# Last output rows of two batches as one tile of 128 rows, and a new order of all instruction lists

## The chip, the cores and the metric

The kernel runs on one core of one Trainium2 chip. The core has a matrix engine (TensorE, "PE" in the profile, with its weight loads as "PEld"), a vector engine (DVE), a scalar engine (ACT), GpSimd (POOL), a queue for transfers (SyncE, "SP"), and 16 DMA engines that move data. The engines run their own lists of instructions, each list in its order, and wait for one another by semaphores. The metric is the device time of one execution in microseconds, as the median of several runs.

## The reference

Eight batches, eight heads, 576 positions, 64 features a head. First a linear attention with cosine weights, then a gated long convolution of the attention's output:

```
# attention, per batch and head
theta = pi/2 * pos / S
phi(x) = concat(relu(x)*cos(theta), relu(x)*sin(theta))      # 128 features
kv  = phi(k)^T v            # 128 x 64
z   = sum_s phi(k)          # 128
att = phi(q) kv / (phi(q) z + 1e-6)

# gated convolution, per batch; x = att with heads side by side: 576 x 512
x1, x2, x3 = split(x @ w_proj)                               # 512 -> 3 * 512
x2_conv    = irfft(rfft(x2, n=S) * rfft(filter_fft, n=S))    # along the 576 positions
out        = (x1 * x2_conv * x3) @ w_out                     # 576 x 512, float32
```

## The kernel before, in words

All matrix products are in float16 with float32 sums in PSUM. PSUM is used in four units of 4 KB a partition (`unit`, line 69); every product goes into a unit, and an eviction (`ev`, line 131, on ACT, or on DVE where the plan says so) or a DVE operation empties it. The next product but three needs that unit again.

For each batch b the work is cut into steps, each with a two- or three-letter name:

- `Lq`, `Lk`, `Lv`: loads of q, k, v (`load_rows`, line 156) from POOL's queue, which turn float32 into float16. There are six raw buffers, so a load of batch b waits until batch b-2 has been used.
- `pk`, `pq` (lines 505 and 519): the products relu(k)·cos, relu(k)·sin and those of q, in pieces, on DVE, or on ACT where the word has `'a`. `va` copies v.
- `kv` (line 556): kv and z by 40 small matmuls. `qt` (573): q's features transposed, by PE for batches 0 and 1 and by a DMA transpose from SP's queue after that. `num` (600): numerator and denominator, then three DVE operations that end in `att`.
- `fx` (629): the folding of positions that begins the Fourier transform. `xp` (666) and `xt` (659): att transposed, by PE for batches 0 to 2, by a DMA transpose for batches 3 to 7. `pr` (676): x2 = the folded att times w_proj, the largest 512-column products. `dft` (701), `mul` (718), `inv` (765): transform, product with the filter's spectrum, inverse transform.
- `ga`, `gb` (730): x1 and x3 from xt and w_proj, 8 matmuls of 288 columns for each of four blocks. `g` (751): their product.
- `y` (786): the last steps of the inverse transform and the product with the gates. It leaves `y` for rows 0 to 511 of the batch in four groups of 128 columns, and `ye` for the last 64 rows.
- `out` (837): the output product. `out b.0` and `out b.1` make two tiles of 128 rows each, evict 128x1024 float32 and store two times 256 KB. `out b.2` is for the last 64 rows (`left`, line 853): since 64 rows fill half of the array, columns 0 to 255 go to partitions 0 to 63 and columns 256 to 511 to partitions 64 to 127, by two matmuls of 256 columns for each of four blocks of the sum; then a 128x256 eviction and two stores of 64 KB. Batch 7 is done tile by tile (`end`, line 863).

The order is written out by hand: a text of words (line 905), and `run` (line 890) takes the next step of each word's generator when the word comes. So `out0.2` in three places means: matmuls, eviction, store. `*3` means three steps, `'a` ACT, `'v` DVE, and `~` that a load is held until the last DVE operation and transpose issued so far. Each engine's list is the order in which the words name its steps.

Buffers that matter here: `att`, `xt`, `y`, `ye` and `g` two each; `os` (the output of a full eviction) three; `os4` (that of the last rows) one.

Of the kernel before, what the change touches and what calls it, by code (L numbers as in the profile page):

```python
# [11 lines left out]
FP32 = mybir.dt.float32  # L12
FP16 = mybir.dt.float16
# [4 lines left out]
def kernel(  # L18
# [19 lines left out]
    nc = tc.nc  # L38
# [3 lines left out]
    B, NH, S, D = q.shape  # L42
    DM = NH * D
    NJ = 5
    NP = 96
    NC = DM // 128
# [7 lines left out]
    OUTSC = 2.0 ** -29  # L54
# [5 lines left out]
    NM = NC * 128  # L60

# [5 lines left out]
    late = {}  # L67
# [26 lines left out]
    wo16 = const("wo16", [128, NC, DM], FP16)  # L94
# [691 lines left out]
    def step_y(b, c, n):  # L786
# [10 lines left out]
        if "y" not in moe[b]:  # L797
# [9 lines left out]
            out=ym[:, :, :, 0:128], in0=ym[:, :, :, 0:128],  # L807
# [3 lines left out]
        if "ye" not in moe[b]:  # L811
            moe[b]["ye"] = late["p"].tile([128, NC, 64], FP16, tag="ye", bufs=2, name=f"ye{b}")
        tt(
            out=moe[b]["ye"][:, c : c + n].rearrange("p c (a t) -> p c a t", t=4),
# [5 lines left out]
    def out_tile(b, t, dst, cs):  # L820
        y = moe[b]["y"]
        for c in cs:
            if t < 4:
                nc.tensor.matmul(  # L824
                    dst, y[:, c, ds(QS * t, 128)], wo16[:, c], start=(c == 0), stop=(c == NC - 1),
                )
                continue
            for hf in range(2):
                nc.tensor.matmul(
                    dst[ds(64 * hf, 64), 0 : DM // 2], moe[b]["ye"][:, c],  # L830
                    wo16[:, c, ds(hf * (DM // 2), DM // 2)], start=(c == 0), stop=(c == NC - 1),
                )
# [20 lines left out]
    def left(b, u):  # L853
        os_ = late["p"].tile([128, DM // 2], FP32, tag="os4", bufs=1, name=f"os{b}_4")
# [35 lines left out]
    def run(plan, **batch):  # L890
# [15 lines left out]
        cols io0 pad1 Sk0.0 pad2 cols io2 rows io1 cols rows th tf warm0.12 cols*5 Sv0.0  # L906
        rows pad0 th'v rows*3 th'v cols*3 rows pk0.0'a*2 rows pk0.0'a*2 tf pk0.0 rows
        pk0.0'a tf pk0.0 cols*2 rows va0.1 cols ones0 rows*2 pk0.0*2 rows va0.0'v pk0.0'a
        th'v Lq0.0 Lq0.1 kv0.0 rows pq0.0 pq0.0'a*4 pq0.0 pq0.1*2 qt0.1 pq0.1*3 Lk0.1 qt0.0
        pq0.1'a qt0.2 kv0.0 qt0.1'b num0.1 tf pk0.1'a pk0.1*3 tf pk0.1 qt0.0'c num0.0 pk0.1  # L910
        ones1 pk0.1'a pk0.1*2 Lv0.1 va0.2 num0.0 num0.1 pk0.1'a va0.3'v qt0.2'b Lw0 kv0.1*2
        num0.1 num0.0 num0.1 cols Lw2 num0.0 qt0.3 rows Lq1.2 num0.2*2 cols*2 xp0.0 qt0.3'b
        rows num0.2 rows num0.2 Lk1.2 xp0.0*2 xp0.0'a num0.3*4 xp0.1 Lv1.2 ga0.0 gb0.3 Lw1
        xp0.1*2 pad4 cols pad5 ti xp0.1'v cols pad3 Lf gb0.0*2 tf ga0.0 gb0.0 ga0.0 Lf
        gb0.3*2 ga0.3 gb0.2 ti tf th ~Lq2.2 cols ~Lk2.2 cols pq1.2*2 pq1.2'a pq1.2*2 pq1.2'a
        rows gb0.2 ga0.3 ga0.1*2 ga0.3'v ti cols fx0.1 fx0.0 pk1.2 gb0.2 pk1.2 gb0.1*2 ga0.1
        fx0.3 fx0.1 pk1.2*2 fx0.0'v ga0.2 pk1.2 fx0.2 th gb0.1 fx0.3 fx0.2 ga0.2*2 pk1.2
        tf'v pk1.2*4 qt1.0 va1.0'v kv1.2 va1.1'v kv1.2 th kv1.2 qt1.1 g0.0.2 qt1.0'v th
        ~Lq3.1 tf qt1.0'v qt1.1'v qt1.2 qt1.1'v qt1.2 ~Lk3.0 qt1.2 num1.0*3 tf pr0.1 th
        num1.1 num1.0 num1.2 g0.2.2 num1.1 tf ~Lq3.0 num1.2 num1.1 pr0.1 tf ti pr0.0 num1.2  # L920
        num1.1 qt1.3 num1.2 pr0.0 pr0.2 qt1.3 dft0.0 feo0 pr0.2 dft0.0 feo1 h0 qt1.3'v xp1.0
        ti xp1.0 pq2.2 fx1.1 pq2.2 h0'v h1 ~Lv2.2 pq2.2 xp1.0 pq2.2 pk2.2 xp1.0'v pk2.2
        pk2.2'a h0 fx1.1 pk2.2 num1.3*3 pq2.2 num1.3 pq2.2 qt2.3 h2 qt2.0 fx1.2 h1 pk2.2 h1
        pk2.2 xp1.1 fx1.3 xp1.1 ~Lk3.1 ~Lq4.1 ~Lv3.1 h2 fx1.2 xp1.1'v fx1.3 xp1.1'v fx1.0
        pk2.2*2 dft0.1 dft0.1'v ~Lo dft0.2 ga1.0 fx1.0 dft0.2 mul0 ti mul0 pr1.0 pr1.2 ti*2
        mul0 ga1.0 mul0 pr1.1 pr1.1'v pr1.0 ga1.0 inv0.1 inv0.0 ~Lq4.0 ti pk2.2 late pr1.2
        dft1.2 dft1.0 dft1.2'v inv0.1 dft1.1 pk2.2 inv0.0 inv0.2 va2.0'v dft1.0 kv2.2 pq3.2
        va2.1'v inv0.3 kv2.2 y0.0.2 ~Lk4.1 y0.0.2 dft1.1 inv0.2 ga1.2*2 mul1 gb1.2 mul1
        qt2.1 kv2.2 num2.0 ~Lv3.0 qt2.2 num2.0 inv0.3 num2.1 pq3.2'a ga1.2 gb1.2 ~Lv4.0
        num2.1 num2.0 num2.1 num2.0 num2.1 gb1.3*2 mul1*2 gb1.2 gb1.1*2 pq3.2'a pq3.2 gb1.3  # L930
        pq3.2'a ga1.1 pk3.2 gb1.1 num2.2 ~Lk4.0 num2.2*3 y0.0.2 ga1.1 y0.0.2 fx2.1 y0.2.2
        ga1.1 y0.2.2 gb1.0*2 pk3.2'a fx2.1 inv1.1 fx2.2 pk3.2 gb1.0 inv1.1 fx2.2 ga1.3
        y0.2.2 ga1.3 inv1.0 inv1.0'v ga1.3 xp2.0 num2.3*3 xp2.0*3 num2.3 pk3.2 inv1.3*2
        y0.0.2 inv1.2*2 fx2.0*2 fx2.3*2 g1.0.2 ga2.0 xp2.1*2 pr2.0 xp2.1*2 pq3.2 ga2.0
        y0.2.2 qt3.0 va3.0'v y1.0.2 pk3.2 pk3.2'a*2 pk3.2 y0.2.2 pk3.2'a pq4.2 pr2.1 ga2.0
        qt3.2 pq4.2 out0.0 pr2.2 pr2.1 pr2.0 out0.0 dft2.1 y1.0.2 dft2.0 ~Lq5.0 va3.1'v
        y1.0.2 ~Lq5.1 ~Lv4.1 y1.0.2 pk3.2 ~Lv5.0 qt3.1 y1.2.2*2 pr2.2'v dft2.1 y1.2.2 dft2.2
        kv3.2*2 y1.0.2 gb2.1 y0.2.2 gb2.1 dft2.0 g1.2.2 y0.0.2 pq4.2'a ~Lv5.1 qt3.3 dft2.2'v
        kv3.2 gb2.0*2 mul2*2 num3.0*4 ~Lk5.0 gb2.1 gb2.0 gb2.3 pk4.2'a gb2.3*2 ~Lk5.1 out0.2
        ga2.2*2 fx3.0 out0.2 pq4.2'a ga2.1 mul2*2 ga2.2 fx3.0 num3.1*2 num3.2*2 pk4.2'a  # L940
        ga2.1 num3.1 pk4.2 out0.1 num3.2 num3.1 y1.2.2 ga2.1 num3.2 num3.3*2 pk4.2 pk4.2'a
        num3.3*2 ga2.3 gb2.2 ga2.3 xt3 pq4.2'a gb2.2 out0.1 fx3.1 fx3.2 ga2.3 inv2.1 gb2.2
        fx3.3 pq4.2 qt4.0 qt4.1 pk4.2'a pk4.2*2 fx3.3 fx3.1'v fx3.2'v inv2.1 pk4.2'a inv2.0
        pk4.2 inv2.0 g2.2.2 qt4.2 va4.0'v va4.1'v y2.0.2*2 pr3.0*2 pr3.1 pq5.2 pr3.1 kv4.2
        g2.0.2 y1.2.2 ~Lk6.0 ~Lq6.0 kv4.2*2 pq5.2'a pr3.2 ga3.0 pk5.2 pr3.2'v pk5.2 y1.2.2
        ga3.0 inv2.2 out0.2 dft3.2 ~Lk6.1 inv2.2'v dft3.0*2 dft3.2'v dft3.1*2 num4.0 inv2.3
        pk5.2*2 inv2.3 num4.0 y1.0.2 pq5.2'a gb3.1 num4.1 num4.0*2 num4.2 mul3 gb3.1 num4.1
        ~Lq6.1 pq5.2'a out1.0*2 num4.2 num4.1 pq5.2'a qt4.3 num4.1 ga3.1*2 pq5.2'a y2.0.2
        num4.2 gb3.0 num4.2 y2.0.2 y2.2.2 num4.3 gb3.0 num4.3 out0.0 out1.1*2 y2.2.2 num4.3
        gb3.3 fx4.0 qt5.2 num4.3 fx4.2 gb3.2 mul3 xt4 gb3.3'v ga3.2 qt5.1 mul3 pk5.2 fx4.0  # L950
        fx4.2 mul3 fx4.1 g3.0.2 inv3.0 qt5.0 gb3.2 qt5.3 fx4.3 y2.2.2 ga3.2 fx4.1 pk5.2*3
        inv3.0'v fx4.3 pk5.2 inv3.1 inv3.1'v y2.2.2 y3.0.2*2 pk5.2'a pr4.0 y3.0.2 inv3.3
        pr4.0 y2.2.2 inv3.3 out1.2*2 pr4.2 out1.2 pr4.1 y3.0.2 ~Lq7.0 va5.0'v kv5.2 y2.0.2
        va5.1'v pr4.1'v inv3.2 pq6.2 pr4.2 kv5.2 ga4.0 pk6.2*2 ~Lv6.1 ga4.0'v inv3.2 kv5.2
        out0.1 dft4.2 pq6.2 pq6.2'a*2 pq6.2 dft4.1 dft4.0 ga3.3 dft4.2 dft4.0'v pk6.2 dft4.1
        mul4 ~Lq7.1 num5.0*3 ga3.3 ~Lv6.0 num5.0 ~Lk7.1 gb4.1 num5.1*2 g3.2.2 pk6.2'a*2
        out2.0 gb4.1 y3.2.2 out1.0 out2.0 pk6.2'a pk6.2 pk6.2'a gb4.0 num5.1 gb4.0 num5.1
        out2.1 mul4 num5.2 ~Lk7.0 ga4.1 ga4.2 out2.1 fx5.1 num5.2 y2.2.2 num5.2*2 num5.3*4
        ga4.1 ga4.2 fx5.0 fx5.1 fx5.2 fx5.0 y2.0.2 gb4.2 gb4.2'v mul4 fx5.3 fx5.2 out2.2
        fx5.3 va6.0 pq6.2'a g4.0.2 pr5.2 pr5.2'v pk6.2'a pr5.0*2 out2.2 y3.2.2*2 pr5.1 mul4  # L960
        pk6.2'a va6.1'v pr5.1'v inv4.1*2 y3.2.2 inv4.0 inv4.3 dft5.1 xt5 inv4.0 inv4.3 qt6.0
        dft5.2 pq7.2 dft5.0 ga5.0 dft5.1 dft5.2'v pq7.2*2 y3.2.2 y4.0.2 y3.2.2 dft5.0 out1.1
        inv4.2 pq7.2 kv6.2*2 y3.0.2 mul5 out2.0 gb4.3 inv4.2 pk7.2 kv6.2'v y4.0.2*3 y4.2.2
        ga5.0 qt6.1 out3.0 mul5 gb4.3 pk7.2'a pk7.2 pk7.2'a y3.0.2 gb5.1 ga4.3 out3.0 num6.0
        ~Lv7.0 num6.0 num6.1*2 num6.0 num6.1 num6.0 gb5.1 ~Lv7.1 pq7.2 out3.1 qt6.2 pq7.2'a
        ga4.3 out3.1 num6.1 y4.2.2 ga5.3 g4.2.2 ga5.3 ga5.2 num6.2 qt6.3 ga5.1 num6.2*2
        ga5.2 ga5.1 num6.3 num6.2 num6.3*2 gb5.0 fx6.0 gb5.2 y4.2.2 pk7.2'a num6.3 gb5.0
        pk7.2'a fx6.2 mul5 fx6.1 fx6.0 fx6.2 gb5.3 mul5 xt6 gb5.2'v g5.0.2 fx6.3 fx6.1
        va7.0'v pk7.2 inv5.0 fx6.3 inv5.0 gb5.3 y4.2.2 pr6.1 g5.2.2 inv5.2 y4.2.2 pr6.1
        pk7.2 ga6.0 inv5.1 out3.2 qt7.2 inv5.2 va7.1 ga6.0'v pr6.2 pr6.0 inv5.1'v out2.2  # L970
# [48 lines left out]
```

## Time and profile before

| | before |
|---|---|
| time, median of 3 runs | 224.58 us (223.02 to 225.03) |
| span of the profiled run | 222.9 us |
| last matmul ends | 217.05 us |
| L829, last rows | 64 matmuls of 256 columns, 5.0 us busy |
| evictions of the last rows | 7 on ACT, 386 ns each; 1 on DVE, 425 ns |
| stores of 64 KB | 15 from SP (2.3 us to landing), 1 from ACT |
| stores of 256 KB | 30 from SP (3.2 us to landing), 2 from ACT |
| xt transposes | 5, from 4.8 to 9.7 us to landing |

How to read the profile: a line of the page's first part gives each engine's busy time. The second part cuts the span into 40 slices of 5.57 us; a digit is the busy share in tenths. In a timeline, the columns are start, length, engine, line, operation, what is written from what, and in square brackets how long the engine stood idle before it and what ended that idle time. The chain of waits goes back from the last instruction to what released it, step by step; its columns are start, length, and what ran. Matmuls overlap, so their mean length is more than the distance from one start to the next; the chain shows the distance.

### The profile page before, as it was taken

To read this page: it belongs to the slowest core of one execution; us is meant where nothing else is said; L and a number is where in the kernel's file an instruction comes from. 1 tells how busy PE (TensorE), PEld (TensorE's weight loads), DVE (VectorE), ACT (ScalarE), POOL (GpSimd) and SP (SyncE) were. 2 spreads that over 40 slices of the span, in tenths; PEclk is the share of its full clock that TensorE was granted. 3 is DMA by queue.
4 is the path that set the end of the run, shared out by engine and by line. 5 is a ranking of instruction groups with operands and counts; after the bars stand their busy time and mean duration, and the time that the engine had idled before them with its cause. 6 is when DMAs were issued, how large, how long until landed. Compare 5 with 4: busy or idle time off the path is not lost.

```text
span 222.9 us, 5869 instructions
## 1 busy us (share of the span) xinstructions
PE 207.7 (93%) x2316; PEld 142.8 (64%) x2316; DVE 194.7 (87%) x473; ACT 170.7 (77%) x275; POOL 65.5 (29%) x105
## 2 busy tenths in 40 slices
PE   7388989999999999999999999799999999999990
PEld 2176776574888476756686667476876667477630
DVE  7998999989999989989999997889888797589930
ACT  4796989998898999888784975877787736476651
POOL 8892456213962096003500184002200000000000
PEclk9979999999999999999999999999999999999996
DMA  5999999999999999999999999997999940823084
GB/s 170 190 186 192 191 209 193 175 138 210 144 189 184 173 161 182 169 195 163 170 157 194 200 199 182 146 300 156 110 177 149 326 132 3 197 94 138 22 258 165
DMA packets 90907, 38.39 MB, mean 172 GB/s; under 512 B 58944, under 2 KB 86592, under 8 KB 90880
## 3 DMA queue, kind: packets, MB, share of 16 engines
q0 software_dynamic: 38944, 16.26, 59.8%
q1 hardware_dynamic: 51568, 21.17, 46.0%
q10 hardware_dynamic: 368, 0.59, 0.7%
q8 instruction: 18, 0.29, 0.5%
q14 instruction: 9, 0.07, 0.1%
HBM read 33.69 MB, written 9.44 MB: 193 GB/s over the span
## 4 chain that ended last, share of the span: by engine, by line
PE 67%; DVE 14%; DMA 10%; ACT 3%; issue 2%; POOL 2%; ACTq 0%; DVEq 0%; POOLq 0%
PE x L736 22%; PE x L680 11%; PE out L824 10%; DMA xt<-att 4%; PE kv L563 4%; PE num L606 4%; PE dft L711 3%; PE fx L634 3%; DMA out_dram<-os 3%; DMA raw<-in_q_dram 3%; PE inv L770 3%; PE inv L774 2%; DVE kp L111 2%; DVE yf L116 2%; DVE qp L111 2%
## 5 line engine op out<-in xcount | busy, mean ns | idle before, releaser
L736 PE MATMUL x<-xt,wp 128*128 128x288 f16 x512 | 71.2, 286 | 0.6 <-DMA xt<-att 0.3
L736 PEld LDWEIGHTS <-wp 128*128 128x128 f16 x512 | 47.9, 98 | 15.8 <-issue 2.8
L680 PE MATMUL x<-wp,fx 128*128 128x512 f16 (+1 forms) x160 | 34.6, 381 | 0.0
L824 PE MATMUL out<-wo,y 128*128 128x512 f16 x128 | 30.1, 379 | 0.0
L138 ACT ACTIVATE os<-out 128x1024 f32<-128x1024 f32 (+2 forms) x24 | 18.3, 767 | 12.5 <-PE out L824 10.1
L116 DVE TENSOR_TENSOR att<-num,rcp 128x640 f16<-128x640 f32 x32 | 26.0, 819 | 0.6
L680 PEld LDWEIGHTS <-fx 128*128 128x128 f16 (+1 forms) x160 | 13.6, 100 | 15.0 <-issue 2.1
L138 ACT CAST x0s<-x 128x576 f16<-128x576 f32 x27 | 17.2, 641 | 6.0 <-PE x L736 5.1
L138 ACT CAST x2s<-x 128x576 f16<-128x576 f32 x28 | 17.8, 639 | 4.8 <-PE x L736 4.7
L138 ACT ACTIVATE x2f<-x 128x1024 f16<-128x1024 f32 (+1 forms) x18 | 16.2, 903 | 6.6 <-PE x L680 5.6
L158 POOL DMA_DIRECT2D raw<-in_q_dram x14 | 11.2, 797 | 31.4 <-ACT x0s L138 18.2
L824 PEld LDWEIGHTS <-y 128*128 128x128 f16 x128 | 12.1, 98 | 12.6 <-issue 0.4
L138 ACT CAST fx<-fx 128x576 f16<-128x576 f32 x29 | 17.8, 648 | 1.8 <-PE fx L640 1.5
L138 ACT CAST eq<-inv 128x576 f16<-128x576 f32 x26 | 16.0, 648 | 3.9 <-PE inv L774 3.3
L158 POOL DMA_DIRECT2D raw<-in_k_dram x13 | 10.5, 811 | 27.0 <-DVE rcp L617 14.6
L770 PE MATMUL inv<-itab,yf 128*128 128x144 f16 x128 | 16.9, 226 | 1.2 <-ACT x2f L138 0.9
L158 POOL DMA_DIRECT2D raw<-in_v_dram x13 | 10.5, 805 | 21.8 <-DVE rcp L116 17.3
L774 PE MATMUL inv<-itl,yf 128*128 128x288 f16 x64 | 16.8, 286 | 0.0
L563 PE MATMUL kv<-va,kp 128*128 128x65 f16 x320 | 12.4, 193 | 4.0 <-DVE va L134 3.8
L563 PEld LDWEIGHTS <-kp 128*128 128x128 f16 x320 | 11.6, 98 | 5.8 <-ACT kp L514 4.0
L606 PEld LDWEIGHTS <-qpt 128*128 128x128 f16 x320 | 13.0, 98 | 3.6 <-issue 0.9
L606 PE MATMUL num<-kvs,qpt 128*128 128x65 f16 x320 | 14.3, 194 | 0.9 <-ACT qpt L138 0.5
(163 smaller groups left out, 432.8 us busy)
## 6 DMA issues: line engine op xcount, KB each, us to landing
out_dram<-os SPq DMA_DIRECT2D x30, 256.0 KB, 3.2
raw<-in_q_dram POOLq DMA_DIRECT2D x12, 256.0 KB, 6.9
raw<-in_k_dram POOLq DMA_DIRECT2D x11, 256.0 KB, 7.2
raw<-in_v_dram POOLq DMA_DIRECT2D x11, 256.0 KB, 6.5
wp<-in_moe_w_proj_dram POOLq DMA_DIRECT2D x3, 512.0 KB, 8.6
raw<-in_q_dram POOLq DMA_DIRECT2D x2, 512.0 KB, 12.1
raw<-in_k_dram POOLq DMA_DIRECT2D x2, 512.0 KB, 13.3
raw<-in_v_dram POOLq DMA_DIRECT2D x2, 512.0 KB, 10.5
```

What stands on the lines that cost most here:

```text
L111: last_dve[0] = nc.vector.tensor_scalar(out=out, in0=in0, scalar1=s1, scalar2=s2, op0=op0, **({"op1": op1} if op1 else {}))
L116: last_dve[0] = nc.vector.tensor_tensor(out=out, in0=in0, in1=in1, op=op)
L138: return nc.scalar.copy(out=out, in_=in_) if mul is None else nc.scalar.mul(out=out, in_=in_, mul=mul)
L158: first = queue.dma_start(out=rw[:, to, 0 : 4 * D], in_=src[b, hs, 0:NM].rearrange("h (p j) d -> p h (j d)", j=4),)
L563: nc.tensor.matmul(u[:, g, ds((h % 4) * 65, 65)], kp[:, j, h].rearrange("p a b -> p (a b)"), va[:, h, j, 0:65], start=(j == 0), stop=(j == ...
L606: nc.tensor.matmul(u[:, hh, ds(t * 65, 65)], qpt_buf[:, h, ds(t * 128, 128)], kvs[:, h // 4, ds((h % 4) * 65, 65)], start=True, stop=True,)
L634: nc.tensor.matmul(uf[:, ds(256 * t, 144)], att[:, c, t], fm.rearrange("p v a -> p (v a)"), start=(t % 2 == 0), stop=False,)
L680: nc.tensor.matmul(dst, fx[:, c, ds(128 * ch, n)], wp16[:, c, ds(DM, DM)], start=(c == cs[0]), stop=(c == cs[-1]),)
L736: nc.tensor.matmul(u[:, hf, 0:HS], wp16[:, i, ds(w * DM + c * 128, 128)], xt[:, i, ds(HS * hf, HS)], start=(i == 0), stop=(i == NC - 1),)
L770: nc.tensor.matmul(u[:, comp, ds(par * QS, QS)], yf[:, comp, ds(par * DM + c * 128, 128)], itab[:, par + 4 * comp], start=(par == 0), stop ...
L774: nc.tensor.matmul(u[:, comp, 0:HS], yf[:, comp, 2 * DM : NF], itl[:, c, comp].rearrange("p a b -> p (a b)"), start=False, stop=True,)
L824: nc.tensor.matmul(dst, y[:, c, ds(QS * t, 128)], wo16[:, c], start=(c == 0), stop=(c == NC - 1),)
```

## The change

Two things. First, the last 64 rows of batches 0 and 1, 2 and 3, 4 and 5 are put side by side in one `ye` tile of 128 columns, so that one product makes the last rows of both batches, with all 128 rows of the array and 512 columns: 4 matmuls of 512 columns instead of 16 of 256, one eviction of 128x512 instead of two of 128x256, and two stores of 128 KB instead of four of 64 KB. It is done with the later batch of a pair. Batches 6 and 7 stay as they were. Second, the text of words, and with it the order of every engine's list and the choice of ACT or DVE for many evictions and products, is a new one throughout.

```
+    BP = B - 2
...
         if "ye" not in moe[b]:
-            moe[b]["ye"] = late["p"].tile([128, NC, 64], FP16, tag="ye", bufs=2, name=f"ye{b}")
+            if b < BP and "ye" in moe.get(b ^ 1, {}):
+                moe[b]["ye"] = moe[b ^ 1]["ye"]
+            else:
+                moe[b]["ye"] = late["p"].tile([128, NC, 2, 64], FP16, tag="ye", bufs=2, name=f"ye{b}")
...
+            if b < BP:
+                nc.tensor.matmul(
+                    dst, moe[b]["ye"][:, c].rearrange("p b n -> p (b n)"), wo16[:, c],
+                    start=(c == 0), stop=(c == NC - 1),
+                )
+                continue
...
     def left(b, u):
-        os_ = late["p"].tile([128, DM // 2], FP32, tag="os4", bufs=1, name=f"os{b}_4")
+        os_ = late["p"].tile([128, DM], FP32, tag="os4", bufs=1, name=f"os{b}_4")
+        if b < BP:
+            ev(os_, u[:, 0], OUTSC)
+            yield
+            for x in range(2):
+                nc.sync.dma_start(out=out[b - 1 + x, NM:S], in_=os_[ds(64 * x, 64)])
+            yield
+            return
```

Of the words, four places. The start, before:

```
        rows pad0 th'v rows*3 th'v cols*3 rows pk0.0'a*2 rows pk0.0'a*2 tf pk0.0 rows
        pk0.0'a tf pk0.0 cols*2 rows va0.1 cols ones0 rows*2 pk0.0*2 rows va0.0'v pk0.0'a
        th'v Lq0.0 Lq0.1 kv0.0 rows pq0.0 pq0.0'a*4 pq0.0 pq0.1*2 qt0.1 pq0.1*3 Lk0.1 qt0.0
        pq0.1'a qt0.2 kv0.0 qt0.1'b num0.1 tf pk0.1'a pk0.1*3 tf pk0.1 qt0.0'c num0.0 pk0.1
```

and after:

```
        rows*3 pad2 cols rows cols rows*3 pk0.0*2 va0.0'v pad5 pk0.0'a rows cols pq0.0
        pq0.0'a cols pq0.0'a pq0.0 pq0.0'a pq0.0 qt0.1 Lq0.1 pq0.1 pq0.1'a cols Lk0.1 pq0.1
        pk0.0 qt0.0 pk0.0'a tf pk0.0'a pq0.1 qt0.1'b cols rows cols pq0.1 pq0.1'a tf pk0.0
        pk0.1 pk0.1'a kv0.0 qt0.2 qt0.0'c kv0.0 num0.0 cols num0.1 pk0.1'a pk0.1*3 tf
```

The end, before:

```
        inv7.2 y7.0.2 y7.2.1 out5.0 y7.2.1 y7.3.1*2 y7.2.1*2 ga7.3 out6.0 out6.1 y6.0.2
        y7.2.1 gb7.3 out6.2 out5.2 out6.1 y7.3.1*2 g7.3.1 y7.3.1 end0*2 end3 end0 out6.0
        end2 out6.1 out6.2 end1 y7.2.1 end1*3 end2 y7.0.2 end4 y7.3.1 end4 end0 end2 end3*3
        out6.2 end2 end4'v end4
```

and after:

```
        inv7.2 y7.0.2*2 inv7.3*2 y7.0.2 y7.3.1 out6.0 inv7.2 y7.3.1 y7.2.1*2 y7.0.2 y7.2.1
        out6.1 y7.2.1 out5.0 y7.3.1 y7.0.2 out6.0 out6.1 gb7.3 y6.2.2 out6.2 y7.2.1 end0
        y7.3.1 end1 gb7.3 g7.3.1 y7.3.1 end0 out6.2 end3 out6.0 out6.1 y7.3.1 end1 out6.2
        end0'v end0 y7.2.1 end1'v end4 end1 end4 end4'v end2 end4 end2 end2'v end2 end3
        end3'v end3
```

## Prediction, written before the result was known

> **What bounds the kernel now.** I read first the busy time of each engine, then the span in forty slices.
>
> ```profile
> PE 207.7 (93%) x2316; PEld 142.8 (64%) x2316; DVE 194.7 (87%) x473; ACT 170.7 (77%) x275; POOL 65.5 (29%) x105
> ...
> PE   7388989999999999999999999799999999999990
> ...
> DVE  7998999989999989989999997889888797589930
> ACT  4796989998898999888784975877787736476651
> ```
>
> PE is full from slice 6 on, with one dent (the 7 at 145 to 150 us); DVE is nearly as full in the first half and has air in the second. Busy PE is modelled, so I price PE by the spacing of its starts in the chain of waits: 16 gate matmuls in 1.96 us (0.1225 each), 8 of 512 columns in 1.73 (0.216), 40 of kv in 1.27, 10 of num in 0.31, four plus two of fx in 0.39, 24 of dft in 1.09, six of inv in 0.49, 8 of L829 in 0.56. Times their counts, with 7.8 us of transposes, 3.7 of filter products and 5.3 of warm-up: about 200.5 us of PE work between 1.19 us and the last matmul's end at 217.05. So PE stands still some 15 us: about 7.6 in the first 25 us, 3.2 from 25 to 60, 1.9 from 60 to 140, 1.8 from 140 to 150, and nearly nothing after. Then 5.9 us pass without PE. An order of instructions can win only in these places.
>
> Next, the dent. This is the timeline around it:
>
> ```profile
> 139.94 1.26 ACT L138 COPY va<-raw 128x1280 f16<-128x1280 f16 x1 [1.99 <-DMA raw<-in_v_dram]
> ...
> 142.34 1.00 ACT L138 ACTIVATE x2f<-x 128x1024 f16<-128x1024 f32 x1
> ...
> 143.39 0.28 PE L770 MATMUL inv<-itab,yf 128*128 128x144 f16 x2 [0.93 <-ACT x2f L138]
> ```
>
> A copy of v of batch 6 waited 2 us on ACT for its load; the x2 eviction behind it came late; PE waited 0.93 us for the PSUM unit which that eviction frees. The chain in the same place shows a second late arrival, the transpose of att of batch 5:
>
> ```profile
> 135.91 0.60 PE x L736 x5
> 136.51 9.66 DMA xt<-att
> ...
> 146.22 1.15 PE x L736 x8
> ```
>
> The window 140 to 145 has 3.81 us of PE busy; with the small gaps at 144.8 and 146.2 the dent costs about 1.2 us.
>
> Last, the end of the chain:
>
> ```profile
> 214.45 3.50 DMA out_dram<-os
> ...
> 218.04 0.61 ACT os L138
> 218.64 0.42 DVE os L111
> ```
>
> PE is done at 217.05, but the last full eviction needs the third buffer of `os`, which is free when the store issued at 214.45 has landed (217.95). Then come an eviction, another, and a store: 222.9.
>
> **What the Trainium skill says.** "TensorE: Matmul & The Clock Gate", section "The mechanism" of its Part 3: matmuls on different column groups of the array run at the same time, each at a few ns from the other. The trace agrees: L829 uses two groups of 64 columns, and its 8 matmuls of 256 columns, 273 ns each, take 0.56 us on PE, where eight one after the other at 0.216/2 would take 0.86. "Perfetto Trace Analysis", section "Identifying the Most-Contended Engine": PE's busy share is a poor measure of headroom; here 93% busy hides 15 us, as shown. "DMA: Bandwidth & Descriptors", section "Issuing engines are not separate DMA queues": transfers from all engines share the 16 DMA engines and interleave. The trace agrees: the five xt transposes land 4.8, 9.6, 9.7, 4.9 and 5.0 us after issue, and the two long ones come right behind bursts of loads by POOL (103.7 to 109.1, and 127.3 to 137.4 us).
>
> **The change, part by part.**
>
> *Last rows in pairs.* Batches 0 to 5: per pair two times 0.56 us on PE become four matmuls of 128 rows by 512 columns, 4 x 0.216 = 0.86. That is 0.26 a pair, 0.8 us for three; two of the old groups took only 0.44 in the chain, so the bounds are 0.1 and 0.8; I take 0.6. PE is the bound there, so it counts. Six evictions of 386 ns on ACT become three of 597 ns: 0.5 us of ACT, hidden, since ACT is idle a quarter of the time there. Twelve stores become six, about 0.55 us of issue each: 3.3 us of the SP queue, hidden, except that transposes stand in that queue. The pair's `ye` waits for the later batch; the trace has no such wait. Queued behind the waiting matmuls are gates and x2 on PE. The lists put out1.2, out3.2 and out5.2 after the later batch's `ye` by several microseconds of PE work, so I price it 0; the upper bound is one `y` step on DVE, 0.4 us. The single `os4` buffer now serves five evictions instead of eight: no new wait.
>
> *Loads and transposes.* In the new lists the load of v6 stands 18.9 us of PE work before its copy instead of 11.3 (it landed 8.5 us after issue), and all va copies from batch 1 on are on DVE. The ACT wait and what it caused go: -1.2 us. But xt of batch 4 now has 8.9 us of PE work between the last att and the first gate instead of 10.9, with the load burst just ahead of it as before. If it again lands after 9.6 us, the gate's matmuls wait, and everything behind them on PE: the trace had about 1.7 us to spare, so 0.3 short, up to 1.1; I take +0.5. xt of batches 3, 5, 6 and 7 have 7.2, 9.7, 9.7 and 12.6 us against landings of 4.8, 9.7 and 5.0: at most a tenth or two.
>
> *Start.* Up to the first long run of gates (22.17 us) PE waits for DVE and ACT. The new order transposes q first and does kv0.0 third. ACT takes one piece of q of the second half, whose data land at 11.1, ahead of two pieces of k, and DVE has one more k piece and a few small operations before the first rcp. So the first att starts about 0.9 us later than 16.21. Against that, both xt copies go to DVE, and PE gets four x2-gate matmuls (0.49 us) to do in the following wait. Net +0.3, between -0.7 and +1.
>
> *Balance.* By the rows' means DVE gets 5.4 us more and ACT 5.3 less (three x2 evictions of 1.22, five va copies or casts, four last output evictions of 0.69, against five k products of 0.35, three gate casts and four small ones back). At each batch's kv the new lists have, for the same PE work, DVE and ACT work within 1 us of before up to batch 5; from batch 6 DVE has 2 to 3 us more, where the trace has DVE idle for over 10 us between 150 and 200. So 0.
>
> *End.* The last gate now comes behind out6.1, and five evictions of batch 7 stand on DVE. PE ends inv7 at 207.1, out6.1 at 210.5, the last gate at 211.5; ACT reaches its cast at 211.6; g and y follow at 213.1 on DVE, where before they were done at 213.18. The first block of batch 7 is out of PSUM at 214.4 as before, so its store lands at 217.95 and the last eviction (now DVE, 0.69) again waits for it: 218.7 instead of 219.06 for the last of them, then the store. -0.35. On DVE the eviction of block 0 stands ahead of the last `ye`, so the last-rows matmuls of batch 7 wait some 0.5 us, and block 2 behind it on PE; both still end before 217.95, so this costs 0.
>
> Sum: -0.6 - 1.2 + 0.5 + 0.3 - 0.35 = -1.35 us. 224.58 - 1.35 = 223.2.
>
> **Rivals.** *Faster:* the new order also takes away most of the scattered idle of PE from 25 to 140 us (5.1 us). For it: every such gap is a PSUM unit or an operand that came a few tenths late, which another order can move. Against it: in 25 to 60 us DVE and ACT are both over 90% busy, and their joint work up to batch 2's kv is equal within 0.6 us in both lists. If 2.5 us of it goes and xt4 is on time: 223.2 - 2.5 - 0.5 = 220.2.
>
> *Slower:* the lists lose at the joints. xt4 1.1 short, the start 1.0 late, a DVE that is 5 us fuller and holds PE by 1.5 us more (a copy of v that waits for its load now blocks DVE, and behind it all att, y and yf work), and the dent not gone but moved, for example q4, whose second half is now loaded 7.7 us of PE work before its use instead of 18.8. Then 224.58 - 0.6 + 1.1 + 1.0 + 1.5 - 0.35 = 227.2. Against it: DVE's distance for q4 is still about 11 us, against a median landing of 6.9.
>
> *No change:* the dent's 1.2 us goes, but comes back at other joints: 224.4.
>
> **How the numbers follow.** Forecast 0.45, faster rival 0.25, no change 0.13, slower rival 0.17. A measurement tells 1%, 2.2 us: faster means below 222.3. From the forecast, with +-1.5 us about it, a third lies below that. So faster 0.25 + 0.15 = 0.40; slower 0.17 + 0.02 = 0.19; the rest, 0.41, is within 1%. The range goes from a little below the faster rival, 219.8, to the slower one, 227.0.
>
> **What would show it.** L829 down to 16 matmuls, three evictions of 128x512; no ACT or DVE wait for in_v near 140 us and no PE gap over 0.3 us at the inverse transforms of batch 4; a PE wait for xt at the first gate of batch 4, if I am right there; the first run of gates starting at 22.2 to 22.8; the last matmul at about 216, and the last eviction again behind a store. It is wrong if a load or a transpose stands late in front of DVE's or PE's queue (2 us at once), or if PE's scattered gaps between 25 and 140 us shrink or grow by more than 1.5 us.

## The result, and the profile after

The changed kernel takes 225.46 us (median of 13 runs) and the kernel before 223.60 on the same chips: a ratio of 1.0079, 95% interval 1.0052 to 1.0105. The change makes the kernel slower by 0.8%, 1.8 us; 1.35 us faster was forecast. The first three runs of the kernel before (median 224.58) and its profiled execution (224.69 us) lay 1 us or more above the medians that later runs gave (223.2 to 223.6).

From the page of the changed kernel, the busy times and three rows of the forty slices (span 223.5 us):

```profile
PE 207.0 (93%) x2280; PEld 142.0 (64%) x2280; DVE 200.7 (90%) x476; ACT 165.7 (74%) x269; POOL 64.0 (29%) x105
...
PE   6288989999899999999999999999999999999980
...
DVE  7788999999999999998999996999999995979962
ACT  4587698999889987879795977588976536377710
```

The dent at 145 us is gone, DVE has 6 us more and ACT 5 less, as counted; the list of PE's waits is empty from 60 to 217 us. But PE is emptier at the left edge, and DVE has 6 and 2 tenths in the last two slices, where it had 3 and 0. A table of three stretches shows where the traces differ:

| | before | after |
|---|---|---|
| first transform of batch 0 starts | 39.83 | 41.21 |
| from there to the end of the last matmul | 177.22 | 175.90 |
| from there to the end | 5.85 | 6.39 |

So 1.38 us are lost at the start, 1.32 won in the middle, 0.54 lost at the end. That is +0.6. Of the other 1.2 us, 1.1 are what the trace of before has over its median, and the rest is about what the trace of after lies under its own.

**The start.** The first key-value sum and the first `att`, in the timeline of before:

```profile
9.72 0.80 PE L563 MATMUL kv<-va,kp 128*128 128x65 f16 x20 [3.23 <-DVE va L134]
...
16.21 0.82 DVE L116 TENSOR_TENSOR att<-num,rcp 128x640 f16<-128x640 f32 x1
```

and the chain of waits of the changed kernel over the same time (start, length, what ran):

```profile
5.30 5.74 DMA raw<-in_q_dram
...
11.13 0.49 DVE qp L112
...
12.14 0.13 DVE kp L112
...
13.25 0.55 DVE kp L112
...
13.94 1.04 PE kv L564 x16
14.98 1.07 PE qt L587 x10
16.05 1.11 PE num L607 x20
```

The sum over the first half of k (`kp`) is in this chain behind a load of q. No data joins them: the second half of q lands at 11.0 us, DVE has waited 0.51 us for it, and two pieces of k, whose data had landed by 4.9 us, stand behind it in DVE's list. The sum ends at 15.0 instead of 10.5, and the first `att` comes at 18.11.

**The end.** The timeline after the last matmuls of the changed kernel (their end: 217.11 us):

```profile
213.38 1.12 SPq L878 DMA_DIRECT2D out_dram<-os  x2
...
216.12 0.39 ACTq L895 DMA_DIRECT2D out_dram<-os  x1
217.58 1.62 DVE L112 TENSOR_SCALAR os<-out 128x256 f32<-128x256 f32 x3 [1.49 <-DMA out_dram<-os]
...
219.23 0.34 ACTq L895 DMA_DIRECT2D out_dram<-os  x1
```

DVE waits 1.49 us until the last rows of batch 6, issued at 213.38, have left the only `os4` buffer, and two full evictions whose matmuls are done stand behind it. In the kernel before that eviction waited too (4.84 us), but it was the last instruction of DVE, and the full ones were on ACT.

### The profile page after: what moved, and what is told of

Same layout as the page of the kernel before. It is cut to its first block, busy times and chain, and to the rows that moved or that the text cites. A ratio compares the mean times of both kernels' runs of the same rounds, so it can differ in the third digit from the quotient of the medians.

```text
span 223.5 us, 5781 instructions
## 1 busy us (share of the span) xinstructions
PE 207.0 (93%) x2280; PEld 142.0 (64%) x2280; DVE 200.7 (90%) x476; ACT 165.7 (74%) x269; POOL 64.0 (29%) x105
## 4 chain that ended last, share of the span: by engine, by line
PE 78%; DVE 10%; DMA 4%; ACT 2%; POOL 2%; issue 1%; DVEq 1%; SPq 0%; POOLq 0%; ACTq 0%
PE x L737 25%; PE x L681 13%; PE out L830 11%; PE kv L564 5%; PE num L607 4%; PE inv L771 4%; PE dft L712 3%; PE inv L775 3%; PE fx L635 3%; DVE kp L112 3%; DMA raw<-in_q_dram 3%; DVE qp L112 2%; DMA out_dram<-os 2%; PE fx L641 2%; PE qt L587 1%; PE xp L671 1%
## 5 line engine op out<-in xcount | busy, mean ns | idle before, releaser
L139 ACT CAST x0s<-x 128x576 f16<-128x576 f32 x30 | 19.1, 642 | 8.6 <-PE x L737 8.3
L159 POOL DMA_DIRECT2D raw<-in_q_dram x14 | 11.8, 845 | 43.0 <-ACT xf L139 15.3
L139 ACT CAST eq<-inv 128x576 f16<-128x576 f32 x27 | 16.6, 651 | 5.5 <-PE inv L775 4.9
L139 ACT ACTIVATE os<-out 128x1024 f32<-128x1024 f32 (+2 forms) x16 | 14.5, 903 | 7.5 <-PE out L830 6.0
L139 ACT ACTIVATE x2f<-x 128x1024 f16<-128x1024 f32 (+1 forms) x14 | 12.5, 903 | 8.5 <-PE x L681 8.3
L139 ACT CAST xf<-dft 128x1024 f16<-128x1024 f32 (+1 forms) x20 | 15.6, 832 | 0.7 <-PE dft L712 0.7
L564 PE MATMUL kv<-va,kp 128*128 128x65 f16 x320 | 13.0, 198 | 3.1 <-DVE kp L112 1.6
L607 PEld LDWEIGHTS <-qpt 128*128 128x128 f16 x320 | 13.8, 100 | 2.7 <-ACT qpt L139 0.6
L607 PE MATMUL num<-kvs,qpt 128*128 128x65 f16 x320 | 14.9, 197 | 0.4 <-ACT qpt L139 0.4
L564 PEld LDWEIGHTS <-kp 128*128 128x128 f16 x320 | 12.1, 101 | 4.9 <-DVE va L135 2.0
```

What stands on the lines that cost most here:

```text
L139: return nc.scalar.copy(out=out, in_=in_) if mul is None else nc.scalar.mul(out=out, in_=in_, mul=mul)
L159: first = queue.dma_start(out=rw[:, to, 0 : 4 * D], in_=src[b, hs, 0:NM].rearrange("h (p j) d -> p h (j d)", j=4),)
L564: nc.tensor.matmul(u[:, g, ds((h % 4) * 65, 65)], kp[:, j, h].rearrange("p a b -> p (a b)"), va[:, h, j, 0:65], start=(j == 0), stop=(j == ...
L607: nc.tensor.matmul(u[:, hh, ds(t * 65, 65)], qpt_buf[:, h, ds(t * 128, 128)], kvs[:, h // 4, ds((h % 4) * 65, 65)], start=True, stop=True,)
```

## The experiments

Ratios are to the kernel before, from runs on the same chip, with 95% intervals.

| run | us | ratio |
|---|---|---|
| e1, longer warm-up | 224.17 | 1.0025 (1.0007 to 1.0044) |
| e2, old start | 223.38 | 0.9990 (0.9976 to 1.0004) |
| e3, old end | 225.97 | 1.0096 (1.0063 to 1.0128) |
| e4, pairs alone | 224.92 | 1.0053 (1.0029 to 1.0077) |
| e5, k first | 223.50 | 0.9998 (0.9981 to 1.0016) |
| e6, own buffer | 224.28 | 1.0031 (1.0012 to 1.0050) |
| e7, before with two `os4` | 223.64 | 1.0008 (0.9987 to 1.0028) |
| e8, pairs alone, own buffer | 224.98 | 1.0073 (1.0050 to 1.0096) |
| e9, k first and own buffer | 222.73 | 0.9964 (0.9943 to 0.9985) |
| e10, and shared end buffers | 222.23 | 0.9937 (0.9915 to 0.9960) |
| e11, new order without pairs | 225.79 | 1.0102 (1.0061 to 1.0142) |
| e12, before with e10's end | 223.63 | 1.0020 (1.0001 to 1.0039) |
| e13, before, longer warm-up | 223.96 | 1.0019 (0.9996 to 1.0041) |
| e14, own buffer, longer warm-up | 224.11 | 1.0038 (1.0020 to 1.0056) |

**e1: the clock.** The page's row of granted clock (tenths of full speed, one digit a slice) begins 9758 after and 9979 before, so the clock was the first suspect.

```diff
-        pad4 pad3 cols pad1 warm0.12 io2 ...
+        pad4 pad3 cols pad1 warm0.24 io2 ...
```

> The changed kernel with 24 warm-up matmuls instead of 12, so that TensorE is not idle for 4.25 us between the warm-up and the first transposes of q. Theory 1 (the start loses, because the longer idle stretch drops the granted clock: 0.50 in 10 to 15 us and 0.66 in 15 to 20): the clock in these windows comes back to 1.00, the first division of the numerators starts about 1 us earlier than 18.11, and the time falls from 225.5 by about 1.0 us, a ratio of about 1.003 to 1.004 to the kernel before. Theory 2 (the start waits for data through VectorE and the loads, the clock is only a sign of it): clock up, but first division within 0.3 us of 18.1 and the ratio stays at 1.008. Theory 3 (the loss is made in the middle or at the end): first division earlier, but the ratio stays at 1.008.

The busy time of each engine by stretches of 5 us (PE, PEld, DVE, ACT, POOL, then the granted clock, the DMA share and GB/s), for the changed kernel and then for e1:

```profile
10.00:15.00 5.00, 3.75 (x43) 3.46 (x44) 4.46 (x21) 3.89 (x8) 5.00 (x7) 0.50 1.46 191
```

```profile
10.00:15.00 5.00, 3.19 (x43) 2.76 (x44) 4.44 (x21) 3.87 (x9) 5.00 (x7) 0.66 1.45 186
15.00:20.00 5.00, 4.50 (x79) 4.31 (x77) 3.94 (x18) 3.83 (x8) 1.71 (x4) 0.66 1.30 204
```

The clock rose from 0.50 to 0.66 here, and not at all from 15 to 20 us, where the changed kernel has 0.66 too; the first `att` came at 18.08 against 18.11, the last matmul ended at 217.06 against 217.11. Still the median fell by 1.3 us. In its trace the whole gain is at the end: the store of `os4` landed 2.13 us after issue instead of 3.56, before DVE came for the buffer, and from the last matmul to the end it is 5.2 us instead of 6.39. e14 asks about this below.

**e2: the old start.** The lists begin as before up to the fourth step of `num0.3` and go on in the new order.

```diff
-        pad4 pad3 cols pad1 warm0.12 io2 ... (new, to num0.3)
+        cols io0 pad1 Sk0.0 pad2 cols io2 ... (old, to num0.3)
```

> The changed kernel whose lists begin as in the kernel before, up to the fourth numerator step of the first part, and then go on in the new order. Theory 1 (the start is the loss): the first division is back at 16.2, the lead of about 1.4 us is kept to the end, ratio about 1.002. Theory 3 (the middle or the end): the lead at 25 us is used up by the later waits (the second and third batch's key-value sums), ratio 1.006 to 1.008.

223.38: the start is worth 2.1 us. The transform of batch 0 starts at 38.72, and the lead of 2.5 us over the changed kernel is 2.7 at the last matmul's end (214.39).

**e3: the old end.** The last 70 steps in the old order, the full evictions on ACT again.

```diff
-        ... end0'v end0 y7.2.1 end1'v end4 end1 end4 end4'v end2 ... end3'v end3
+        ... end0*2 end3 end0 out6.0 end2 ... out6.2 end2 end4'v end4
```

> The changed kernel whose lists end as in the kernel before, from the last gate product of batch 7 on (the last 70 steps). Theory of the tail (three last evictions stand on VectorE behind one that waits 1.49 us for the store of the same buffer): time from the last matmul to the end falls from 6.4 us to 5.8 and the ratio to about 1.005. Rival (both ends wait for the same stores and the same last matmuls): no change, 1.008.

No gain. From the last matmul to the end 6.36 us (6.39): the eviction of the last rows holds nobody up, but ACT now waits 0.87 us for a full buffer. That the two evictions stand on DVE is not the loss by itself. But the test is not a clean one: the store that ACT waits for took 4.11 us to land, the same store in the old order 3.47 to 3.50 (before, e7, e12), and this alone is about what the old end would have won (see the last section).

**e4: the pairs alone**, in the order before.

```diff
 (the changed kernel's code for ye, out_tile and left; the order before)
-        out0.2 (3 times), out2.2 (3), out4.2 (3)
```

> The kernel before with the last rows of two batches as one tile and nothing else: its order, without the steps of the three tiles that are gone. As forecast for this part: 12 matmuls of 512 columns take 2.6 us where 48 of 256 took 3.3, TensorE is full there, so -0.6 us, ratio 0.997 (bounds 0.1 to 0.8 us). Rival 1 (the pairs cost a wait for both batches' rows or for their one output buffer): ratio 1.002 or more. Rival 2 (order is all that counts, the matmuls' time is refilled by waits): 1.000.

1.2 us slower: a miss. Compare the trace with e7's, which has the old code and order up to the end. At the place of the second batch's tile, first e7 and then e4:

```profile
119.33 0.63 PE L829 MATMUL out<-wo,ye 128*64 128x256 f16 x8
119.79 2.43 PE L680 MATMUL x<-wp,fx 128*64 128x512 f16 x12
```

```profile
118.55 1.03 PE L835 MATMUL out<-wo,ye 128*128 128x512 f16 x4
119.50 2.46 PE L681 MATMUL x<-wp,fx 128*64 128x512 f16 x12
```

Here the pair takes 0.95 us of PE's time (119.50 - 118.55) for the old tile's 0.46 (119.79 - 119.33), half a microsecond more. The gain must come where the partner was taken out, and there the list of PE's waits from 83 to 95 us has, in e4 alone,

```profile
PE fx L635 <- DVE att L117: 0.7, 1, 0.7
```

which e7 doesn't have: the 0.56 us set free at batch 0's tile became a wait for DVE. The starts of the transforms show it for all three. At batch 2's transform e4 is 0.69 us ahead of e7. This lead stays through the removal of batch 0's tile, shrinks by 0.43 at the first pair (from 102 to 125 us), stays through the removal of batch 2's (125 to 145), shrinks by 0.42 at the second pair, grows by 0.43 where batch 4's goes (172 to 196) and loses 0.50 at the third. Two of three savings didn't reach the next transform. From the transform of batch 0 to the last matmul e4 takes 176.50 us and e7 175.44. The rest is at the end, where ACT waits for full buffers:

```profile
211.11 3.46 SPq L862 DMA_DIRECT2D out_dram<-os  x4
...
215.82 0.60 ACT L139 ACTIVATE os<-out 128x512 f32<-128x512 f32 x1 [1.64 <-DMA out_dram<-os]
```

The four stores take SP 3.46 us to issue (2.54 in e7), and the one that ACT needs lands 4.17 us after issue (2.73 in e7). What goes with the slow landing is a transfer of instructions that falls among these stores in e4 and before them in e7; the last section has it. From the last matmul to the end e4 and e8 take 0.7 to 1.0 us more than e7 and e12, so about half of what the pairs cost in the old order lies at the end, and not in their work on PE.

**e5: k first.** Five steps of the start moved, nothing else.

```diff
-        ... pk0.0'a rows cols pq0.0 ... pk0.0 qt0.0 pk0.0'a tf pk0.0'a ... pk0.0 ... kv0.0
+        ... pk0.0'a rows cols pk0.0 pk0.0'a*2 pk0.0 kv0.0 pq0.0 ... qt0.0 tf ...
```

> The changed kernel with five steps of its start moved and nothing else: the last four scaled pieces of the first half of k, which stood on VectorE and ScalarE behind the pieces of q, and the first key-value sum itself, stand ahead of q again. Theory 1a (order: the sum waits for k pieces that wait behind the late q loads): the sum starts at about 9.7 us instead of 12.5, its last matmuls do not wait 1.00 us for VectorE, the first division comes at about 16.5 instead of 18.1, and the time falls by 1.5 to 2 us: ratio 0.999 to 1.001, as with the whole old start. Theory 1b (the clock, because the pads stand ahead of the warm-up's zeros, or the longer gap): the clock stays at 0.5 to 0.8 and less than 0.7 us is won, ratio 1.005 or more.

It gives back 2.0 us, all of what e2 gave. In its timeline

```profile
9.59 1.30 PE L564 MATMUL kv<-va,kp 128*128 128x65 f16 x17 [0.57 <-ACT kp L515]
...
16.31 1.56 DVE L117 TENSOR_TENSOR att<-num,rcp 128x640 f16<-128x640 f32 x2
```

the sum ends at 10.9 and `att` comes at 16.31; the transform of batch 0 starts at 39.28 (41.21), and the last matmul ends at 215.13 (217.11). The pads and the late warm-up stayed where they were; the clock is back at 1.00 from 15 to 20 us without more warm-up, and PE has work from 8.6 on. So the start's loss is the order of k and q on DVE and ACT, and the low clock went with it.

**e6: an own buffer for the last rows of batch 7**, and **e7**, a control on the kernel before.

```diff
+        if b == B - 1:
+            os_ = late["p"].tile([128, DM // 2], FP32, tag="os4e", bufs=1, name=f"os{b}_4")
+        else:
             os_ = late["p"].tile([128, DM], FP32, tag="os4", bufs=1, name=f"os{b}_4")
 (e7, in the kernel before:)
-        os_ = late["p"].tile([128, DM // 2], FP32, tag="os4", bufs=1, name=f"os{b}_4")
+        os_ = late["p"].tile([128, DM // 2], FP32, tag="os4", bufs=2, name=f"os{b}_4")
```

> The changed kernel with an output buffer of its own for the last rows of batch 7, so that its eviction does not wait for the store of batch 6's. Theory of the tail: the wait of 1.49 us on VectorE goes, the two evictions behind it come 0.7 to 1 us earlier, time -0.7 to -1.0, ratio 1.004. Rival (the evictions then wait for the stores of the other output buffers, and the stores land one after another anyhow): less than 0.3 us, ratio 1.007.

> The kernel before with a second buffer for the tiles of last rows, as a control of the one above. If the buffer alone sets the end there too: the last eviction, on VectorE at 218.64 behind 4.84 us of waiting, comes at about 217, and the last big eviction at 218.04 still waits for its own store: -0.4 us, ratio 0.998. Rival (the last big eviction sets the end): 1.000.

e6 wins 1.2 us. In its timeline the two evictions no longer stand behind the last rows:

```profile
215.14 1.02 DVE L112 TENSOR_SCALAR os<-out 128x512 f32<-128x512 f32 x2
...
216.88 0.69 DVE L112 TENSOR_SCALAR os<-out 128x512 f32<-128x512 f32 x1 [0.71 <-PE out L830]
...
217.85 0.69 DVE L112 TENSOR_SCALAR os<-out 128x512 f32<-128x512 f32 x1 [0.29 <-DMA out_dram<-os]
```

The last starts at 217.85 instead of about 218.5, and from the last matmul to the end it is 5.45 us instead of 6.39. In the kernel before a second buffer changes nothing: there the last rows' wait held nobody up. Together with e1 and e3 the loss is this: a wait put in front of other work in an in-order list. How long it is depends on when the store lands; in e1, with the same list and the same single buffer, it was gone.

**e8: pairs alone with an own buffer**, e4 and e6's edit together.

> The kernel before with the pairs alone and a buffer of its own for the last rows of batch 7. The pairs alone came out 1.2 us slower although the last matmul came 0.5 us earlier in their trace. If the one buffer of the last rows, which now holds twice the bytes, is what costs: ratio 0.998 to 1.000. If it is the three buffers of the big output tiles and their stores (1.64 and 1.31 us of waiting in that trace): 1.004 to 1.006 as before.

1.0073: the buffer of the last rows isn't what the pairs cost in the old order; ACT waits 1.32 us for a full buffer again, and the stretch to the last matmul is 176.28 us.

**e9 and e10: both cures, and shared buffers at the end.** e9 is e5 with e6's edit. e10 also has

```diff
-        os_ = late["p"].tile([128, 2, DM], FP32, tag="os", bufs=3, name=f"os{b}_{t}")
-        ev(os_[:, 0], u[:, 0], OUTSC)
+        if ("os", t // 2) not in moe[b]:
+            moe[b]["os", t // 2] = late["p"].tile([128, 2, DM], FP32, tag="os", bufs=3, name=f"os{b}_{t}")
+        os_ = moe[b]["os", t // 2][:, t % 2]
+        ev(os_, u[:, 0], OUTSC)
```

> The changed kernel with both cures: k's last four pieces and the first key-value sum ahead of q, and a buffer of its own for the last rows of batch 7. If the start (-2.0 us) and the end (-1.2 us) are separate losses they add up: 225.5 - 2.0 - 1.2 = 222.3 us, ratio 0.994 to 0.995. Rival (they share one cause, the landing of the stores): no more than the start alone, 0.999.

> The kernel with both cures, and the four last output tiles of batch 7 as halves of two buffers instead of halves of four, so that no eviction at the end waits for the store that frees one of three buffers. In the run with the own buffer the last eviction still stood 0.29 us behind a store and the one before it 0.71 us behind its matmuls. If stores set the end: another -0.3 to -0.5 us, ratio 0.992 to 0.993. Rival (the last matmul and its own eviction and store set it): as with both cures alone, 0.994.

e9: 222.73, 0.8 us under e5, so the losses are separate; that it is 0.8 for the expected 1.2 lies within the intervals. e10, at 0.9937, beats both kernels. Its evictions at the end wait for matmuls alone:

```profile
213.39 1.02 DVE L112 TENSOR_SCALAR os<-out 128x512 f32<-128x512 f32 x2
...
214.92 1.29 DVE L112 TENSOR_SCALAR os<-out 128x512 f32<-128x512 f32 x2 [0.51 <-PE out L830]
```

and the time after the last matmul is 5.11 us.

**e11: e9's order without the pairs**, the kernel before's code, `os4` twice, and the nine steps of three tiles put back.

```diff
+        out0.2 (14, 24 and 32 steps after the last step of y0; so for out2.2, out4.2)
```

> The order with both cures, but the last rows of each batch as tiles of their own as in the kernel before: the three tiles of batches 0, 2 and 4 are put back, their matmuls some fifteen steps after the rows are ready. Theory A (TensorE is full, so the pairs save 2 x 0.56 - 0.86 = 0.26 us each): about 0.6 to 0.8 us slower than with both cures, ratio 0.998. Theory B (as the pairs in the old order showed: a pair adds 0.4 us where it stands, and the tile that goes saves its 0.56 us only where nothing else holds TensorE there): within 0.4 us of it or faster, 0.992 to 0.996.

225.79, 3.1 us over e9: more than either theory said, and not a clean measure of the pairs. In its trace PE waits from 130 to 172 us for a transpose, a wait that e9 doesn't have:

```profile
PE num L606 <- DMA qpt<-qp: 1.3, 1, 1.3
```

Where no such wait is, the tile that is back costs 0.66 us between the transforms of batches 2 and 3 (23.06 for 22.40). So in the new order, unlike the old, PE is full where batch 0's tile was, and its removal counts. What the pairs bring in all there stays open.

**e12: the kernel before with e10's end.**

```diff
-        os_ = late["p"].tile([128, DM // 2], FP32, tag="os4", bufs=1, name=f"os{b}_4")
+        os_ = late["p"].tile([128, DM // 2], FP32, tag="os4", bufs=2, name=f"os{b}_4")
 (and e10's edit)
```

> The kernel before with a second buffer for the last rows and the shared halves at the end, as a control: how much of the cure of the end is to be had without the change. If its last eviction is held by the store of a big tile (0.24 us of waiting there): -0.3 us, ratio 0.998. Rival: no change, 1.000, since its end was not the loss.

No gain: these buffers were not what set the old end.

**e13 and e14: the longer warm-up again**, in the kernel before and on e6.

```diff
-        ... warm0.12 ...
+        ... warm0.24 ...
```

> The kernel before with 24 warm-up matmuls instead of 12. If the longer warm-up helps whatever the order (a start whose clock is not let down): -0.5 to -1 us, ratio 0.996. If it only mends what the change broke: 1.000. At 140 us the copy of batch 6's v waits less than 1 us for its load, as in the other traces of this order, if the 1.99 us of the first trace were chance; about 2 us again if they belong to the kernel.

> The changed kernel with the buffer of its own for batch 7's last rows and 24 warm-up matmuls. If the longer warm-up won 1.2 us at the start, the two add up: 225.5 - 1.2 - 1.2 = 223.1, ratio 0.998. If it won only at the end, where the store landed sooner: as with the own buffer alone, 1.003.

Neither gains: e14 is at e6's ratio, e13 at before's. With the store out of the way the longer warm-up is worth nothing that shows in the median, so what e1 won was at the end. e13's profiled execution, at 226.0 us, lies 2.0 us above its median, so its times aren't compared. On the question about 140 us it lies between the two answers: the copy of batch 6's v waits again, 1.47 us.

## Why the prediction was wrong, point by point

Three steps failed: the dent at 145 us was taken for a property of the kernel, the start was priced without what stands behind the late pieces of q, and the end followed the wrong buffer. Against the other traces of the old order, the start cost some 1.2 us (forecast +0.3), the middle about 0.3 (forecast -1.3) and the end about 0.5 (forecast -0.35). That sums to 2.0, near the 1.8 that the medians show.

**The base (-1.2 for the dent).** The step "the ACT wait and what it caused go: -1.2 us" was right against the trace and wrong against the kernel. The copy of batch 6's v in two other executions of the old order, e7 and then e4:

```profile
138.85 1.26 ACT L138 COPY va<-raw 128x1280 f16<-128x1280 f16 x1
```

```profile
138.59 1.26 ACT L139 COPY va<-raw 128x1280 f16<-128x1280 f16 x1
```

No wait where the trace of before has 1.99 us; e8 has none either, e12 0.6. From the transform of batch 4 to that of batch 5 these four take 19.48 to 19.56 us, the trace of before 20.91, 1.4 us more. (The prediction's 1.2 is PE's idle time up to 145 us; the gap of 0.26 at 146.2, which it names too, makes it 1.45.) But the trace of e13 has the wait too:

```profile
141.44 1.26 ACT L138 COPY va<-raw 128x1280 f16<-128x1280 f16 x1 [1.47 <-DMA raw<-in_v_dram]
```

and takes 21.27 us for that stretch. So the wait comes and goes between executions of the same order: it is long in the two that lay 1.1 and 2.0 us above their medians, and short or absent in the four within 0.5 us of theirs. The prediction counted as a gain what a usual execution doesn't lose.

**Start: +0.3 (-0.7 to +1).** The failed step that cost most in the changed kernel. It counted that q comes first and that ACT and DVE have more pieces ahead, and made the first `att` 0.9 us late; it came 1.9 late. What the count missed is that a piece of q in an in-order list waits for its load and holds the k pieces behind it, ready or not. A load late in front of DVE's queue was among the prediction's own signs of being wrong. The granted clock fell along with the waits of PE. The Trainium skill, "TensorE: Matmul & The Clock Gate", in "What's actually happening" of its Part 1, says that the array runs at half rate after an idle window of about 3.4 us and needs as long a busy one to come back. The traces agree with this in part. PE stands still 4.25 us before its first transposes, the granted clock is 0.50 from 10 to 15 us and 0.66 from 15 to 20, and 16 matmuls of kv take 1.04 us, while 20 of kv took 0.80 in before. But the length doesn't fit: before the change the clock fell to 0.66 for one stretch after 3.23 us, and in e1 it is 0.66 in both though no wait of PE in its first 25 us is over 1.8 us. e5 prices all of it at 2.0 us. Some 1.2 of it is loss against the old start (the transform of batch 0 starts at 40.9 to 42.3 us in the changed kernel, e1, e3 and e6, at 39.8 to 40.9 in the five traces of the old start in the old order), the rest is what the cured start gains on the old one.

**End: -0.35.** Wrong: +0.54 in the traces, and e6 shows 1.2 us to be had. The prediction did see an eviction behind a store, but of the wrong buffer: it had the last one wait for the third `os` until 217.95, and did not follow `os4`, of which it says "no new wait". The wait was old; what stood behind it was new. How long DVE waits there also hangs on how late that store lands, which the prediction had no term for.

**Last rows in pairs: -0.6.** A pair takes PE 0.86 us twice and 0.97 once in the chain, near the forecast 0.86. The old tile was priced a little high: to the next matmul of other work it takes 0.46 us three times, 0.53 once and 0.56 twice in before, 3.03 us in all, against 2.69 for the pairs. So the three pairs save PE 0.3 us, half of the 0.6 and inside its bounds. The step "PE is the bound there, so it counts" failed: in the old order only one of three savings reached the next transform, and the pairs cost 1.2 us and more in all (e4, e8), about half of it at the end. In the new order the value is open (e11).

**xt of batch 4: +0.5.** Wrong in the cautious direction: the transposes of att land 4.9 to 7.1 us after issue in the changed kernel (6.6 for batch 4), and PE waits for none.

**Balance: 0.** Open. PE waits 0.99 and 0.64 us for DVE at the key-value sums of batches 1 and 2 (0.6 us and none before), but nothing after 60 us; no run isolates it.

**Middle, taken together.** -0.6 - 1.2 + 0.5 = -1.3 was forecast from the trace and 1.32 came; but two other traces with the old code need 175.4 and 175.7 us for this stretch, so that the new order's 175.9 is no gain. That the two numbers agree is luck.

The slower rival had the right sign, and its start "1.0 late" was near the truth; its other joints (xt4, q4, a fuller DVE) weren't what failed.

## What to carry to other kernels

Look whether the profiled execution stands at the median before pricing its gaps: a wait for a load that one execution shows may be no property of the kernel. When a list is reordered, go through each in-order engine for instructions that wait for a load or a store, and ask what stands behind them that could already run; here two such places cost 2.0 and 1.2 us, and moving five steps and adding 1 KB a partition mended both. Work taken off a full engine counts only where nothing else would hold that engine in the same microsecond. And when an edit changes the number of instructions, look where the transfers of instructions fall before the stores of the end are compared.

## What was not expected of the hardware

The store of 64 KB whose buffer DVE waits for landed 3.56 to 3.65 us after issue in three traces (after, e2, e5), but 2.13 in e1, with the same four stores of 256 KB ahead of it in the queue. What differs is a transfer of another kind. The page of the changed kernel lists, besides the queues of the program's own transfers,

```profile
q8 instruction: 18, 0.29, 0.5%
```

(packets, MB, share of the 16 DMA engines), which are 18 transfers of 16 KB, each about 0.9 us or longer, that bring instructions. The last of them starts at 214.31 us in the changed kernel, among the stores of the end, and at 210.14 in e1, ahead of them. The DMA views of 214 to 215 us of the changed kernel and of 210 to 211 us of e1 show it:

```profile
q1 hardware_dynamic: 211, 0.30, 88.3%
q8 instruction: 1, 0.02, 6.1%
```

```profile
q8 instruction: 1, 0.02, 8.2%
```

In all sixteen traces together 28 stores issued after 198 us have such a transfer start between 0.2 us before their issue and 1.7 us after it, and they took 3.29 to 4.41 us to land. The other 235 took 1.93 to 3.50, half of them under 2.6. The slow stores come and go as the edits move the last transfer: 12 more warm-up matmuls bring it 4.2 us forward (e1) or 5.1 (e14, against e6), out of the burst, and without the old tiles' 36 matmuls it comes 6.5 us later (e4, against e7), into it. So this goes with the gain of e1, the end of e4 and e8, and part of the wait at the changed kernel's end. No run moves the transfer and nothing else, so that it holds the stores up is a reading of the traces and not shown by an experiment.

Starts of the same instructions differ from one execution to the next by up to 1 us at 40 us, and the difference can last to the end (the transform of batch 0 at 41.21 us in the changed kernel and 42.25 in e3, whose list is the same up to there, the last matmul's end at 217.11 and 218.14). A difference of a few tenths between the start times of two single traces is therefore no finding.
